# One scatter per tile, a first fold by thirds on VectorE, and tables loaded in the expert stage: one change to a fused attention, experts and Fourier-mixing kernel

## The chip, the cores and the metric

The kernel runs on one core of a Trainium2 chip as one launch. The metric is the device time of that launch in microseconds (us), the median of three runs. A core has five engines with an instruction stream of their own, each in order: TensorE (PE; its weight loads are shown as PEld), VectorE (DVE), ScalarE (ACT), GpSimd (POOL) and SyncE (SP), which here only issues DMA transfers. They meet through semaphores. On-chip data lie in SBUF and PSUM (what TensorE writes); everything else is DRAM.

## What is computed

Three layers over 4 sequences of 576 tokens, 8 heads of 64, model width 512:

```python
# attention: per query only the 32 largest scores are kept
scores = scale * q @ k.T;  kth = the 32nd largest score of each row
attn = softmax(where(scores >= kth, scores, -1e9));  x = attn @ v
# experts: a token's expert is its own argmax, or that of the token before it
e = argmax(logits[b, s]) if s == 0 or local_gate[b, s] < 0.5 else prev_e
out[b, s] = softmax(logits[b, s])[e] * (relu(x[b, s] @ w1[e]) @ w2[e])
# mixing
u = x + real(fft(fft(x, axis=1), axis=2))
un = (u - mean(u)) / sqrt(var(u) + 1e-6)
return u + relu(un @ w_ch1) @ w_ch2
```

All of it is float32. Matrix products are done in three parts: each operand is split into a high part, which TensorE takes without loss, and the rest (low), and high x high, high x low and low x high are added up in PSUM.

## The kernel before

The body is one program with a hand-written order: every engine executes its instructions in the order in which the Python code emits them, and a framework adds the semaphores that the data and the buffers ask for (a buffer of a ring can be written only when its last reader is done).

**Attention** (to about 555 us) ends with each token's row scattered into `xs_d`, sorted by expert. With the row go its weight and, as numbers, the rows of `xm_d` into which its expert's output has to go; they come from a table made in `_tables`. `xm_d` holds per sequence two halves of 289 rows: tokens 1 to 288 and 0 in the one, tokens 575 down to 288 and 0 in the other. The halves are folded later (row n of one with row n of the other), so tokens 0 and 288 stand in both, and a token has up to two target rows.

**Expert stage** (560 to 821 us). Eight experts in order of size, with room for 512, 384, 368, 352, 320, 288, 256 and 256 tokens (`CAPS`); each is 8 steps over the hidden width. A step emits `mm1` (up-projection of 128 hidden units for all tokens of the expert: 12 matmuls, then ScalarE's relu and VectorE's low part) and, two steps later, `mm2` (down-projection into one PSUM bank per tile of 128 tokens, three products). `finish` (L1043) scales the tiles into `ysb`, by ScalarE and VectorE in turn, and `store` (L1058) scatters them with an indirect DMA of GpSimd: per tile two, one for each half of `xm_d`, where the rows without a target in that half are left out by a bounds check; 46 in all. Beside this run: the splitting of the next expert's weights (`raw` to `whi`, `wlo`, L213 and L214), the loads of `xs_d`, the load of the transform's table `tst` (L1094, GpSimd's queue, step 2), and the conversion of the mixing weights, one piece of 128 x 512 in four steps (`f64_step`, L1001: ScalarE L938, VectorE L939 to L946, a store of `fa`, two buffers).

**Transform** (L1183 to L1306). The two-dimensional transform's real part is computed from folded inputs. For each of 4 sequences (batch b): `load_x` brings the two halves `xa` and `xb` in three pieces of 112, 112 and 65 rows (SyncE, two buffers); `fold` makes xa + xb (VectorE: `fe`) and xa - xb (GpSimd: `fo`) and folds each again along the 512 features, first for pieces 0 and 1 together, then for piece 2; `parts` splits both into high and low (`eh`, `el`, `oh`, `ol`). `over_tokens` is one of 5 passes of 9 matmuls with the table `tst` (three from the even fold, two from the odd), each evacuated by ScalarE (high) and VectorE (low) from one of three PSUM buffers. `over_features` is one of 3 blocks of 15 matmuls with the tables `tct` and `tnt`; VectorE's two results go to `md_d`. The next batch's fold is emitted among the passes and blocks of the current one. Ahead of the loop stand the loads of batches 0 and 1, two loads of 1 MB of mixing weights (`m1`), and, on GpSimd behind the first fold, the loads of `tct` and `tnt` (L1280, L1281).

**Mixing** (L1310 on). 2304 tokens in 9 groups of 256. `load_u(g)` brings a group's rows of `md_d` and `xm_d`, and `norm(g)` gives five pieces of work: `add` (GpSimd, two additions into `ut`), `ln` for each half (VectorE with one ScalarE step), and `tr` for each half (four transposes on TensorE, ScalarE's high and VectorE's low part, one PSUM buffer). The hidden width is taken in 4 quarters; a step (quarter q, group g, f) emits `mm1` (12 matmuls), and `mm2` of the step before (6 matmuls; after f = 3 the result is added into `ut`). In quarter 0 the norm of group g + 2 is spread over the steps of group g (f = 3: `add`) and g + 1 (f = 0 to 3: `ln`, `ln`, `tr`, `tr`). The norm of group 0 is done in batch 3 of the transform, its transposes behind feature blocks 0 and 1; group 1's load, norm and transposes come at the head of the mixing:

```python
load_u(1, cp)
nops = norm(1, cp); nops.pop(0)()     # then one piece per step, from step 0
```

## Time and profile before

| | us |
|---|---|
| median of three runs | 1348.8 (1345.58 to 1350.65) |
| the profiled execution, whole | 1346.73 |
| its span (first to last instruction) | 1344.9 |
| busy in the span: TensorE, VectorE, ScalarE, GpSimd | 1210.7, 914.2, 696.3, 572.9 |

The profile is one execution. All its times are counted from the start of the span. A row of the timeline has the start, the duration, the engine, the line, the operation with its output and inputs by tile name, and in brackets how long the engine was idle before it and what ended that. Rows of the chain of waits follow what ended last, backwards. Rows by stage give, for each stretch, the busy time of each engine, the TensorE clock as a share of full speed (0.50 and 1.00 are its two levels, 1.2 and 2.4 GHz), the share of time in which the DMA engines were busy, and what they moved.

### The profile page before, as it was taken

The numbers are of one execution on the slowest core, as the hardware profiler recorded it, in microseconds if no ns is written. First come the engines' busy times: TensorE is split into PE (matmuls) and PEld (weight loads), VectorE is DVE, ScalarE is ACT, GpSimd is POOL, SyncE is SP. The second block draws the span as 40 slices with busy tenths as digits, with TensorE's granted clock in tenths as the row PEclk, the third lists the DMA queues.
The fourth block names the chain that finished last, engine by engine and source line by source line (L and its number), as shares of the span: only waits on it lengthen the run. The fifth ranks groups of instructions, "written<-read, shape, count | busy, mean of one in ns | idle before, by whom it ended". The sixth has DMA issues, their size and how long they took to land.

```text
span 1344.9 us, 25588 instructions
## 1 busy us (share of the span) xinstructions
PE 1210.7 (90%) x8601; PEld 1088.2 (81%) x8601; DVE 914.2 (68%) x3555; ACT 696.3 (52%) x1750; POOL 572.9 (43%) x745
## 2 busy tenths in 40 slices
PE   5999889899899987499999994887999999999996
PEld 4999778888788786389888883776888999999995
DVE  7999899999999997365666673764654444443222
ACT  6999888898899886144444551232322222221110
POOL 5888787987798776302212232642210000000111
PEclk8999989998999899599999997898999999999998
DMA  4656433433444212575666774743230100100111
GB/s 108 184 145 191 121 81 88 109 88 75 101 101 103 50 23 100 187 242 181 216 218 226 229 269 103 211 143 92 83 126 1 62 33 32 63 1 1 48 48 48
DMA packets 128966, 152.29 MB, mean 113 GB/s; under 512 B 69919, under 2 KB 74263, under 8 KB 128712
## 3 DMA queue, kind: packets, MB, share of 16 engines
q1 hardware_dynamic: 122008, 133.34, 34.3%
q0 software_dynamic: 6816, 17.22, 3.7%
q8 instruction: 69, 1.13, 0.3%
q14 instruction: 73, 0.60, 0.1%
HBM read 92.05 MB, written 38.39 MB: 97 GB/s over the span
## 4 chain that ended last, share of the span: by engine, by line
DVE 30%; PE 29%; issue 21%; POOL 11%; DMA 5%; ACT 2%; SPq 1%; POOLq 0%; DVEq 0%; ACTq 0%
PE f L1368 11%; PE f L1352 11%; DVE cd L432 8%; DVE y L463 5%; POOL xm_d L828 4%; DVE sc L469 3%; DMA xs_d<-xtok,ix 3%; PE u L536 2%; DVE cw L443 2%; DVE lo L329 2%; DVE cw L445 1%; POOL y L458 1%; POOL fo L1209 1%; PE s L411 1%; DVE mt L442 1%
## 5 line engine op out<-in xcount | busy, mean ns | idle before, releaser
L432 DVE MAX8 cd<-ss 128x8 f32<-128x72 f32 x1152 | 215.7, 217 | 1.2 <-ACT ss L426 1.0
L1357 DVE SCALAR_TENSOR_TENSOR fhl<-f,fhh 128x256 fp32r<-128x256 f32 x144 | 60.9, 423 | 211.8 <-ACT fhh L1356 211.8
L536 PE MATMUL u<-in_v,et 128*128 128x74 f32 (+1 forms) x1600 | 191.6, 270 | 10.0 <-ACT st_x L543 9.0
L1356 ACT ACTIVATE fhh<-f 128x256 fp32r<-128x256 f32 x144 | 55.3, 384 | 277.4 <-PE f L1352 277.4
L536 PEld LDWEIGHTS u<-in_v,et 128*128 128x128 f32 (+1 forms) x1600 | 182.0, 185 | 19.8 <-ACT st_x L543 15.3
L458 POOL TENSOR_TENSOR y<-ss,g 128x576 f32<-128x576 f32 x144 | 185.1, 1286 | 22.7 <-ACT st_x L543 7.8
L504 POOL TENSOR_TENSOR z<-ss,mt 128x576 f32<-128x576 f32 x144 | 168.7, 1171 | 14.9 <-DVE cd L432 9.8
L1377 POOL DMA_INDIRECT out_dram<-ut,orow x18 | 17.6, 977 | 318.4 <-DVE ut L1373 316.5
L517 PE MATMUL tp<-ident,z 128*128 128x128 f32 x576 | 120.8, 289 | 16.4 <-DVE lo L329 14.7
L453 ACT ACTIVATE g<-ss,mt 128x576 bf16<-128x576 f32 x144 | 118.9, 826 | 29.7 <-DVE mt L446 28.1
L828 POOL DMA_INDIRECT xm_d<-ysb,sid x46 | 49.4, 1073 | 195.9 <-ACT ysb L1052 187.4
L411 PE MATMUL s<-kt,qp 128*128 128x288 f32 x640 | 127.2, 327 | 3.4 <-DVE qp L360 1.6
L495 ACT ACTIVATE bb<-ss,kb 128x576 bf16<-128x576 f32 x144 | 116.7, 810 | 8.7 <-POOL kb L474 8.7
L463 DVE MAX8 y<-y 128x8 f32<-128x576 f32 x144 | 106.7, 741 | 10.9 <-POOL y L458 10.8
L426 ACT ACTIVATE ss<-s 128x288 f32<-128x288 f32 x288 | 111.6, 464 | 4.2 <-PE s L411 2.7
L518 PE MATMUL tp<-neg_id,bb 128*128 128x128 bf16 x576 | 109.3, 224 | 3.9 <-ACT bb L495 3.9
L517 PEld LDWEIGHTS tp<-ident,z 128*128 128x128 f32 x576 | 87.4, 152 | 27.0 <-POOL y L458 7.7
L411 PEld LDWEIGHTS s<-kt,qp 128*128 128x128 f32 x640 | 95.9, 200 | 6.6 <-ACT kt L361 3.1
L1352 PEld LDWEIGHTS f<-nxh,whi 128*128 128x128 f32 x576 | 88.2, 189 | 14.2 <-issue 1.2
L214 DVE TENSOR_TENSOR wlo<-raw,whi 128x1024 fp32r<-128x1024 f32 x70 | 85.5, 1260 | 19.7 <-ACT whi L213 19.5
L1368 PE MATMUL f<-whi,fhh 128*128 128x512 f32 x288 | 92.3, 402 | 0.6 <-ACT fhh L1356 0.6
L1352 PE MATMUL f<-nxh,whi 128*128 128x256 f32 x576 | 91.5, 280 | 1.0 <-DVE dd L1266 1.0
(256 smaller groups left out, 2972.8 us busy)
## 6 DMA issues: line engine op xcount, KB each, us to landing
raw<-in_moe_w_dram SPq DMA_DIRECT2D x32, 1024.0 KB
kt<-hi SPq DMA_DIRECT2D x60, 144.0 KB
kt<-lo SPq DMA_DIRECT2D x60, 144.0 KB
xs_d<-xtok SPq DMA_DIRECT2D x8, 1056.0 KB
fr<-in_moe_w_ch_dram SPq DMA_DIRECT2D x16, 512.0 KB
raw<-in_moe_w_ch_dram SPq DMA_DIRECT2D x16, 512.0 KB
md<-md_d SPq DMA_DIRECT2D x9, 516.0 KB
in_k<-in_k_dram SPq DMA_DIRECT2D x32, 128.0 KB
```

The costliest lines, as they stand in the source:

```text
L411: PE.matmul(p, QP[i][:, s, o:o + 128].bitcast(F32R), KT[i][j][:, s, c].bitcast(F32R), start=(s == heads[0] and j == 0), stop=(s == heads[- ...
L426: ACT.activation(t[:, 288 * hf:288 * hf + 288], SPS.pop((n, hf)), AF.Copy)
L432: return [lambda j=j: DVE.max(cd[:, 8 * j:8 * j + 8], SS[n][:, 72 * j:72 * j + 72]) for j in range(8)]
L453: ACT.activation(g, SS[n], AF.Sign, bias=MT[i][:, t, 1, 7:8], scale=-SCL, accum_out=DIF[n])
L458: POOL.tensor_tensor(y, SS[n], LT[n], op=OP.mult)
L463: DVE.max(y8, Y8[n])
L495: ACT.activation(t, SS[n], AF.Relu, bias=KB.pop(n), scale=-HUGE)
L504: POOL.tensor_tensor(ZZ[n], SS[n], bcast(MT[i][:, t, 0, 0:1], [128, S]), op=OP.subtract)
L517: PE.matmul(o, z[:, k], ident, start=True, stop=False, is_transpose=True)
L536: PE.matmul(p[0:m, s, 0:VW], et[:, kc, qs], vv[:, kc, VC[s]], start=(kc == 0), stop=(kc == 4))
L1352: PE.matmul(p, a[:, d, fs], x[:, d], start=(n == 0), stop=(n == 11))
L1368: PE.matmul(yp[c], a[:, c * 128:(c + 1) * 128], w[:, f, :], start=(f == 0 and n == 0), stop=(f == 3 and n == 2))
```

## The change

1. A token's output goes to one row of `xm_d` only. The table has one target, `store` and the overflow path issue one scatter per tile (23 for 46), and `load_x` reads two halves of 287 rows plus, into both halves, the two rows of tokens 288 and 0.
2. In the last step of an expert `mm2` goes tile by tile instead of product by product.
3. `tct` and `tnt` move to the pool of `tst`; their loads are emitted in the expert stage, at step 10, on GpSimd's queue. To make room `fa` has one buffer.
4. Batch 0 is folded by a new function, `first`: all on VectorE, piece by piece, the even half before the odd one, with ScalarE's high parts between. The load of batch 1 is issued behind the first addition (a transfer of one element that reads its result holds SyncE's queue), and the two loads of mixing weights stand behind the load of batch 2.
5. Groups 0 and 1 are loaded at the start of batch 2 and normalised in batches 2 and 3, their transposes behind passes 2 and 3 and feature blocks 0 and 1 of batch 3. The mixing starts with the load of group 2, and the pieces for group g are placed at steps 4g - 7 (`add`), 4g - 6 and 4g - 5 (`ln`), 4g - 3 and 4g - 2 (`tr`).

```diff
@@ _tables
-                if s <= S // 2:
-                    lay[p, 5 * b + t, 1] = b * 2 * NS + (s - 1) % NS + 1
-                if s == 0 or s >= S // 2:
-                    lay[p, 5 * b + t, 2] = b * 2 * NS + NS + (S - s - 1 if s else NS - 1) + 1
+                lay[p, 5 * b + t, 1] = b * 2 * NS + ((s - 1) % NS if s <= S // 2 else NS + S - s - 1) + 1
...
@@ expert stage
     tst = tp_.tile([112, 3, 4, 290], F32R, name="tst")
+    tct = tp_.tile([128, 3, 2, 258], F32R, name="tct")
+    tnt = tp_.tile([128, 2, 2, 258], F32R, name="tnt")
...
-                FA[i] = mp.tile([128, 512], F32, name="fa", bufs=2)
+                FA[i] = mp.tile([128, 512], F32, name="fa", bufs=1)
...
-            for n, (a, w) in enumerate(((hh, wh), (hh, wl), (hl, wh))):
-                for c in range(nt):
-                    m = min(128, CAPS[r] - 128 * c)
-                    PE.matmul(YP[r][c][0:m], a[:, c * 128:c * 128 + m], w[:, f % 4, :],
-                              start=(f == 0 and n == 0), stop=(f == 7 and n == 2))
+            order = [(n, c) for n in range(3) for c in range(nt)]
+            if f == 7:
+                order.sort(key=lambda o: o[1])
+            for n, c in order:
...
-                for a in range(2):
-                    st = to_rows(sid[0:m, a, c:c + 1], ysb[0:m, c])
+                st = to_rows(sid[0:m, c], ysb[0:m, c])
...
             if j == 2:
                 POOL.dma_start(tst, ts)
+            if j == 10:
+                POOL.dma_start(tct, tcd)
+                POOL.dma_start(tnt, tnd)
@@ transform
+            x = xm_d[2 * b * NS:(2 * b + 2) * NS].rearrange("(g n) d -> g n d", g=2)
             for g, t in enumerate(XA[b]):
-                x = xm_d[(2 * b + g) * NS:(2 * b + g + 1) * NS]
-                SP.dma_start(t[:, 0:2], x[0:224].rearrange("(j p) d -> p j d", p=112))
-                SP.dma_start(t[0:65, 2], x[224:289])
+                SP.dma_start(t[:, 0:2], x[g, 0:224].rearrange("(j p) d -> p j d", p=112))
+                SP.dma_start(t[0:63, 2], x[g, 224:287])
+
+            for t in XA[b]:
+                SP.dma_start(t[63:65, 2], x[0, 287:289])
...
+        def first():
...
+            def add(j, i):
+                m, op = DT[j], (OP.add, OP.subtract)[i]
+                t = fs[i][0:m, j % 2]
+                DVE.tensor_tensor(t, xa[0:m, j], xb[0:m, j], op=op)
+                DVE.tensor_tensor(t[:, 1:256], t[:, 1:256], t[:, 511:256:-1], op=op)
+                ACT.activation((eh, oh)[i][0:m, j], t[:, 0:(258, 256)[i]], AF.Copy)
+
+            def low(j, i):
+                m, n = DT[j], (258, 256)[i]
+                DVE.tensor_tensor((el, ol)[i][0:m, j], fs[i][0:m, j % 2, 0:n], (eh, oh)[i][0:m, j].bitcast(F32), op=OP.subtract)
+
+            for i in range(2):
+                add(0, i)
+                if i == 0:
+
+                    SP.dma_start(fp.tile([1, 1], F32, name="after", bufs=1), fs[0][0:1, 0, 0:1])
+                    load_x(1)
+                add(1, i)
+                low(0, i)
+                add(2, i)
+                low(1, i)
+                low(2, i)
+
         load_x(0)
-        load_x(1)
-        for load, _ in m1:
-            load()
-        for i in range(2):
-            fold(0, i)
-            parts(0, i)
-        POOL.dma_start(tct, tcd)
-        POOL.dma_start(tnt, tnd)
+        first()
         nops = []
         for b in range(B):
             more = b + 1 < B
-            if b == 2:
-                load_u(0, lp)
-            if b == B - 1:
-                nops = norm(0, lp)
+            if b == B - 2:
+                for g in range(2):
+                    load_u(g, lp)
+                n0, n1 = norm(0, lp), norm(1, lp)
+                nops = [n0[:1], n0[1:2], n0[2:3], [n0[3], n1[0]], [n0[4], n1[1]], n1[2:3], n1[3:4], n1[4:5]]
             for c in range(5):
                 over_tokens(b, c)
                 if more and c == 1:
                     fold(b + 1, 0)
-                if len(nops) > 2:
-                    nops.pop(0)()
+                if b == B - 1:
+                    for o in nops.pop(0):
+                        o()
             if b + 2 < B:
                 load_x(b + 2)
+            if b == 0:
+                for load, _ in m1:
+                    load()
             for j in range(3):
                 over_features(b, j)
...
-                if nops and j < 2:
-                    nops.pop(0)()
+                if b >= B - 2 and j == 2 or b == B - 1 and j < 2:
+                    for o in nops.pop(0) if nops else ():
+                        o()
@@ mixing
-        load_u(1, cp)
+        load_u(2, cp)
         steps = [(q, g, f) for q in range(NQ) for g in range(NG) for f in range(4)]
...
+        nops, later = {}, {}
+        for g in range(2, NG):
+            if g > 2:
+                nops.setdefault(4 * g - 9, []).append(lambda g=g: load_u(g, cp))
+            nops.setdefault(4 * g - 7, []).append(lambda g=g: later.update({g: norm(g, cp)}))
+            for k, at in enumerate((7, 6, 5, 3, 2)):
+                nops.setdefault(4 * g - at, []).append(lambda g=g, k=k: later[g][k]())
...
                 if q == 0:
-
-                    if f == 0 and g + 2 < NG:
-                        load_u(g + 2, cp)
-                    if nops:
-                        nops.pop(0)()
-                    if f == 3 and g + 2 < NG:
-                        nops = norm(g + 2, cp)
-                        nops.pop(0)()
+                    for o in nops.pop(i, ()):
+                        o()
```

## Rows read from the trace of the kernel before

**Rows 1.** Busy time by stage (each engine's us and instructions, PE clock, DMA share, GB/s):

```profile
560.00:830.00 270.00, 260.51 (x1409) 225.45 (x1408) 164.08 (x256) 122.63 (x190) 58.49 (x95) 0.98 0.64 215
830.00:849.00 19.00, 6.43 (x23) 5.18 (x24) 8.57 (x9) 2.80 (x6) 11.22 (x9) 0.50 0.98 270
...
1021.00:1345.00 324.00, 312.79 (x2007) 281.89 (x2005) 125.41 (x250) 61.68 (x143) 19.17 (x36) 0.99 0.09 35
```

**Rows 2.** Timeline at the end of the experts: start, us, engine, line, operation:

```profile
820.57 0.63 PE L1040 MATMUL m<-whi,hl 128*128 128x512 f32 x2
...
821.97 0.97 POOL L828 DMA_INDIRECT xm_d<-ysb,sid  x1 [14.72 <-ACT ysb L1052]
```

**Rows 3.** Chain of waits from experts to transform (start, us, what was waited for):

```profile
825.80 2.27 DMA xm_d<-ysb,sid
...
829.40 6.63 DMA xb<-xm_d
```

**Rows 4.** Timeline of the first fold, VectorE beside GpSimd:

```profile
837.40 2.71 DVE L1210 TENSOR_TENSOR fe<-fe 112x510 f32<-112x510 f32 x1
```

**Rows 5.** Instructions by line in the whole span (ns, minimum/median/maximum; first, last start):

```profile
L1208 DVE TENSOR_TENSOR fe<-xa,xb x8: 689/1514/2830, 836.1 to 885.0; 112x1024 f32<-112x1024 f32 x4, 65x512 f32<-65x512 f32 x4
...
L1222 DVE TENSOR_TENSOR el<-fe,eh x8: 424/689/1095, 841.0 to 888.6; 112x516 fp32r<-112x516 f32 x4, 65x258 fp32r<-65x258 f32 x4
```

**Rows 6.** Timeline of the transform: TensorE's first table matmul, batches 1 and 3, GpSimd's fold:

```profile
854.68 0.47 PE L1254 MATMUL pc<-tct,ch 86*112 86x258 f32 x2 [2.52 <-DMA tct<-in_tab_c_dram]
...
861.75 0.44 PE L1240 MATMUL p<-tst,eh 112*86 112x290 f32 x2
...
866.11 2.14 POOL L1211 TENSOR_TENSOR fo<-fo 112x510 f32<-112x510 f32 x1
...
886.97 0.44 PE L1240 MATMUL p<-tst,eh 112*86 112x290 f32 x2
```

**Rows 7.** Timeline of batch 3, three engines:

```profile
891.26 0.43 PE L1240 MATMUL p<-tst,eh 65*86 65x290 f32 x2
...
891.39 0.82 DVE L1243 TENSOR_TENSOR cl<-p,ch 86x290 fp32r<-86x290 f32 x2
892.28 0.69 DVE L1162 BATCH_NORM_STATS2 bs<-ut 128x6 f32<-128x512 f32 x1
...
896.28 0.55 DVE L1169 TENSOR_SCALAR md<-ut,mv,rs 128x512 f32<-128x512 f32 x1
...
891.16 1.09 POOL L1158 TENSOR_TENSOR ut<-ut,md 128x510 f32<-128x510 f32 x1
```

**Rows 8.** Timeline of the mixing's head; TensorE, GpSimd's sum, VectorE's normalisation:

```profile
903.46 0.71 PE L1352 MATMUL f<-nxh,whi 128*128 128x256 f32 x4 [0.99 <-DVE dd L1266]
...
911.05 1.27 POOL L1157 TENSOR_TENSOR ut<-ut,md 128x514 f32<-128x514 f32 x1 [18.80 <-DMA ut<-xm_d]
...
918.18 0.90 PE L1175 MATMUL lt<-ident,md 128*128 128x128 f32 x3 [2.23 <-DVE md L1169]
...
929.76 1.60 DVE L1169 TENSOR_SCALAR md<-ut,mv,rs 128x512 f32<-128x512 f32 x1
...
939.88 0.63 PE L1352 MATMUL f<-nxh,whi 128*128 128x256 f32 x4
...
1018.53 0.63 PE L1352 MATMUL f<-nxh,whi 128*128 128x256 f32 x4
```

**Rows 9.** Timeline of the expert stage: table load, a wait for weights, fa:

```profile
577.20 0.62 POOL L1094 DMA_DIRECT2D tst<-in_tab_s_dram x1
...
589.83 2.01 ACT L213 ACTIVATE whi<-raw 128x1024 fp32r<-128x1024 f32 x2 [4.67 <-DMA raw<-in_moe_w_dram]
...
795.03 0.43 SPq L1012 DMA_DIRECT2D c_d<-fa  x1
...
799.57 0.67 ACT L938 ACTIVATE fa<-fr 128x512 f32<-128x512 f32 x1
```

**Rows 10.** DMA issues (out, in, queue, count, KB each, us from issue to landing):

```profile
tst<-in_tab_s_dram POOLq DMA_DIRECT2D x1, 1522.5 KB, 9.1
```

More of the change, by code (lines that the diff above doesn't have):

```diff
@@ L894, in overflow @@
                 SP.dma_start(xo, xs_d[bass.ds(slot, 128), :])
-                ix = op.tile([128, 2], I32, name="oix")
-                om = op.tile([128, 2], F32, name="om_")
-                rows_of(ix, xo[:, DM + 2 * IW:XW:IW], om)
+                ix = op.tile([128, 1], I32, name="oix")
+                om = op.tile([128, 1], F32, name="om_")
+                rows_of(ix, xo[:, DM + 2 * IW:DM + 2 * IW + 1], om)
                 xt = op.tile([128, 4, 128], F32, name="xt")
@@ L913, in overflow @@
                 ACT.activation(yo, p, AF.Copy, scale=xo[:, DM:DM + 1])
-                for a in range(2):
-                    to_rows(ix[:, a:a + 1], yo)
+                to_rows(ix, yo)
     slow = nc.values_load(slow_i[0:1, 0:1], min_val=0, max_val=1)
@@ L973, in prep @@
             pv = mp.tile([128, XCAP // 128, 1], F32, name="pv", bufs=2)
-            sid = mp.tile([128, 2, XCAP // 128], I32, name="sid", bufs=2)
-            em = mp.tile([128, 2, XCAP // 128], F32, name="em", bufs=1)
+            sid = mp.tile([128, XCAP // 128, 1], I32, name="sid", bufs=2)
+            em = mp.tile([128, XCAP // 128, 1], F32, name="em", bufs=1)
             XH[r] = (xh, xl, pv, sid)
@@ L980, in f @@
                     DVE.tensor_copy(pv[:, 0:nt], XS[r][:, 0:nt, DM:DM + 1])
-                    rows_of(sid[:, :, 0:nt], XS[r][:, 0:nt, DM + 2 * IW:XW:IW].rearrange("p c a -> p a c"), em[:, :, 0:nt])
+                    rows_of(sid[:, 0:nt], XS[r][:, 0:nt, DM + 2 * IW:DM + 2 * IW + 1], em[:, 0:nt])
                 p = ps.tile([128, XCAP], F32, name="tp", bufs=2)
@@ L1036, in mm2 @@
             wh, wl = W[r, f // 4, 1]
-            for n, (a, w) in enumerate(((hh, wh), (hh, wl), (hl, wh))):
-                for c in range(nt):
-                    m = min(128, CAPS[r] - 128 * c)
-                    PE.matmul(YP[r][c][0:m], a[:, c * 128:c * 128 + m], w[:, f % 4, :],
-                              start=(f == 0 and n == 0), stop=(f == 7 and n == 2))
+            order = [(n, c) for n in range(3) for c in range(nt)]
+            if f == 7:
+                order.sort(key=lambda o: o[1])
+            for n, c in order:
+                a, w = ((hh, wh), (hh, wl), (hl, wh))[n]
+                m = min(128, CAPS[r] - 128 * c)
+                PE.matmul(YP[r][c][0:m], a[:, c * 128:c * 128 + m], w[:, f % 4, :],
+                          start=(f == 0 and n == 0), stop=(f == 7 and n == 2))
         def finish(r):
@@ L1061, in store @@
                 m = min(128, CAPS[r] - 128 * c)
-                for a in range(2):
-                    st = to_rows(sid[0:m, a, c:c + 1], ysb[0:m, c])
-                    for o in prev_sc:
-                        tc.declare_no_dep(st.ins, o.ins, reason="every token has its own rows")
-                    prev_sc.append(st)
-                    POOL.memset(spacer, 0.0)
+                st = to_rows(sid[0:m, c], ysb[0:m, c])
+                for o in prev_sc:
+                    tc.declare_no_dep(st.ins, o.ins, reason="every token has its own row")
+                prev_sc.append(st)
+                POOL.memset(spacer, 0.0)
         load_slots(0)
@@ L1185, in body @@
         ps = ph.enter_context(tc.tile_pool(name="dft_ps", bufs=1, space=PSUM))
-        tct = fp.tile([128, 3, 2, 258], F32R, name="tct")
-        tnt = fp.tile([128, 2, 2, 258], F32R, name="tnt")
         XA, FE, EO, CS = {}, {}, {}, {}
@@ L1271, in over_features @@
                 SP.dma_start(md_d[r + NS:r + NS + m, h], dd[0:m, 1 - h])
-        load_x(0)
-        load_x(1)
-        for load, _ in m1:
-            load()
-        for i in range(2):
-            fold(0, i)
-            parts(0, i)
-        POOL.dma_start(tct, tcd)
-        POOL.dma_start(tnt, tnd)
+        def first():
+            EO[0] = [fp.tile([112, 3, n], F32R, name=nm, bufs=1)
+                     for nm, n in (("eh", 258), ("el", 258), ("oh", 256), ("ol", 256))]
+            eh, el, oh, ol = EO[0]
+            xa, xb = XA[0]
+            fs = [fp.tile([112, 2, DM], F32, name=nm, bufs=1) for nm in ("fe", "fo")]
+            def add(j, i):
[17 more added lines that the diff above has]
+                low(2, i)
+        load_x(0)
+        first()
         nops = []
```

3 lines of the change are left out of this document (removed).

## The prediction

> **What bounds the kernel now.** I read the table by stage first [rows 1]. In the expert stage TensorE is busy 260.5 of 270 us and in the last three quarters of the mixing 312.8 of 324, both near full clock: work taken off other engines is worth nothing there. Between experts and transform, 830 to 849, it is busy 6.4 of 19 us at half clock. So the change can pay only in three places: the gap behind the experts, the transform's first batch, and the head of the mixing. The timeline gives the gap: the experts' last matmul ends at 821.2, and the first of four scatters starts at 821.97 [rows 2]. The chain of waits goes on through the fourth, at 825.80, which lands 2.27 us later, and then through the load of xb, issued at 829.40 and landed at 836.03 [rows 3]. The fold follows on VectorE and GpSimd, beside each other, where a step of VectorE's takes up to 2.71 us [rows 4]. TensorE then waits once more, until 854.68, for the table tct; batch 1 starts at 861.75 and batch 3 at 886.97 [rows 6]. The mixing starts at 903.46, idles for the sums and normalisation of group 1 (its sum starts at 911.05, its transposes resume at 918.18) and reaches group 2 at 939.88 and group 8 at 1018.53 [rows 8].
>
> **A. Experts to data.** With the last down-projection sorted by tile, tile 0 is complete three matmuls, about 0.7 us, earlier, so the first scatter starts near 821.3. Four scatters lie (825.80 - 821.97) / 3 = 1.28 us apart; with two, the last starts at 822.55, 3.25 us earlier. It now writes all its rows where it wrote about half: 131 KB more at the 270 GB/s of [rows 1] is 0.5 us, so landing takes 2.7 us (bounds 2.27 and twice that; nearer the first, since most of 2.27 can't be data). Loads then start 2.8 us earlier, at 825.7. Before, the part of batch 0 that the fold needs (1.03 MB) came 7.5 us after the first issue, with 3.2 MB of batch 1 and mixing weights queued behind and sharing the engines. Those are now held back. Alone, 1.03 MB at 270 GB/s is 3.8 us, plus the 2 us that a small transfer shows: 5.8 us (5.5 if it is faster, 7.5 if sharing cost nothing). Data at 831.5 instead of 836.0: **4.5 us** (1 to 5.5). The two extra row loads are 4 KB behind the rest and cost two issues of SyncE with nothing to feed; the mixing weights, moved behind batch 2's load, are needed only in the mixing, and hide under three batches.
>
> **B. First fold.** VectorE now does it alone. Its shortest 512-wide addition is 0.69 us and its shortest 258-wide difference 0.42 [rows 5]; beside GpSimd 510 elements took 2.71 [rows 4]. A third costs 0.69 + 0.42 + about 0.06 of dependence = 1.17, its low part 0.42; three thirds of the even half 4.9, both halves 9.75 us after the data. TensorE's three even passes (1.2 us each at full clock, twice that at half) run beneath the odd half; the two odd ones run from 10.25 to 12.65. VectorE meanwhile evacuates two passes (10.6), folds batch 1's first piece in about 3 beside GpSimd (whose second step takes 2.14 [rows 6], its first no less: 14.3), and evacuates the other three passes: 14.8. Feature block 0 thus ends at 15.0, with tct long loaded, and two more blocks of 1.85 put batch 1 at 18.75 us after the data, where it was 25.7. Batch 1's load is issued behind the first addition, at 1.8, and is in by about 8, before it is wanted at 9.75. The table's removed wait of 2.5 us is not worth 2.5: VectorE's evacuations also ended at 854.6. A and B: batch 1 at 850.25 instead of 861.75, **11.5 us** (7 to 14). Batches 1 and 2 stay at 12.6 each, as measured (25.2 from 861.75 to 886.97): five passes of 1.2, three blocks of 1.85 and a microsecond of waits.
>
> **C. Tables and single buffers in the expert stage.** GpSimd has nothing between the issue of tst at 577.20 [rows 9] and the first scatter, so both tables go out right behind it, not at their step: 1290 KB more while tst takes 9.1 us for 1522 KB [rows 10], 167 GB/s. That is 7.7 us of a shared path. The weights that ScalarE waited for until 589.83 [rows 9] come up to 3.9 us later if they lose half of it. Their result is due at TensorE six or more us after that, so it is covered; uncovered it would cost up to 3. The Trainium skill (DMA: Bandwidth & Descriptors, section "Queues, rings and completion order") says that each DMA engine takes turns between the queues with work; tst's 167 GB/s, on engines that move 270 elsewhere [rows 1], agrees; if the weights went first instead, this part would be 0. The single fa makes ScalarE's next range step wait for the store: in the tightest expert the store is issued at 795.03 and the step starts at 799.57 [rows 9]. 4.5 us against 0.26 MB behind 0.5 MB (2.8 at 270 GB/s, plus 2) is a tie; ScalarE has about 1 us of idle behind it and TensorE a step of 2.8. Loss **0.5 us** (0 to 3). Halving 46 scatters frees GpSimd, which nothing waits for there.
>
> **D. Batch 3 carries two groups.** This is where I expect a loss. VectorE reaches batch 3's first evacuation at 891.39, 4.4 us after the batch began, because GpSimd and VectorE still fold; GpSimd's sum for group 0 ends at 892.25 [rows 7]. So group 0's second normalisation ends no earlier than 896.8 [rows 7], 9.9 us in. TensorE finishes the third pass 4.7 us in [rows 7]. Before, the transposes stood behind the feature blocks; now the first stand between pass 2 and pass 3, and TensorE, in order, has to stand still from 4.7 to about 10. GpSimd's sum for group 1 now runs just then, and such a normalising step took 1.60 us beside GpSimd instead of 0.55 [rows 7, 8]: 10.9 us in. Behind it VectorE is the bound: 0.69 for each transposed half, 0.44 for each evacuation, two normalisations of about 2 us (the first here starts at 892.28, the second's last step ends at 896.83, with one evacuation between [rows 7]) for group 1, with TensorE's half clock after the wait (0.9 us of it on the path): group 1's second ends near 19.5, its first transposes hold feature block 1, and the mixing starts at 25.3 instead of 903.46 - 886.97 = 16.5. **Loss 8.8 us** (4 to 11). Its worth is that groups 0 and 1 are ready.
> The Trainium skill (SBUF — State Buffer, section "Who interferes with whom") says that a VectorE operation using both ports and a GpSimd one block each other wholly, and issue order decides. The 1.60 agrees; if VectorE were first each time, the sum would lose 1 us less.
>
> **E. Head of the mixing.** From 903.46 to group 2 at 939.88 were 36.4 us [rows 8]. A step is 2.8 us (312.8 us of [rows 1] are 111 steps and a half); eight, less the first down-projection, are 21.0, group 2's transposes 0.9, the wait for the last transform stores that the first step keeps 0.6. Group 2's sum can start as group 1's did, 7.6 us behind the first matmul (8.0, one load more); sum and normalisation take 4.4, and the evacuation queued behind it on VectorE comes 1.1 us late. 23.6 us: **12.8 gained** (11 to 13.5). **Then** the order: the transposes waited a step behind a normalisation that GpSimd's sum slowed [rows 8]; now two steps lie between. 24 steps of 2.8 and twelve transposes of 0.46 are 72.8 against 78.65 from 939.88 to 1018.53: **5.85 gained** (4 to 6).
>
> **Sum.** 11.5 - 0.5 - 8.8 + 12.8 + 5.85 = 20.8, on the profiled execution's 1346.7 us (span 1344.9 and 1.8 around it): 1325.9. That execution lies 2.1 below the median of 1348.8, so I predict 1348.8 - 20.8 = **1328 us**.
>
> **Rivals.** (1) The transposes in batch 3 don't hold TensorE, because the fold's end, shifted, leaves VectorE free earlier: D shrinks to about 1 us, 1320. For it: in batch 3 only the fold's tail, 4.4 us, delays the first evacuation; against: that fold is ordered among batch 2's passes, as before, so its tail moves with them. (2) The entrance gains half: the first load is no faster alone and the expert stage loses 3: 11.5 falls to 6, 0.5 rises to 3, 1336. For it: the engines move no more than 270 GB/s in any case. (3) Nothing much: batch 3's wait drops TensorE's clock for the rest of the batch (6 us more) on top of (2): 1343, within the bound of no change. The Trainium skill (TensorE: Matmul & The Clock Gate, section "HAM oscillation") says that an idle TensorE restarts at 1.2 GHz; rows of this kernel agree, the gap of 830 to 849 standing at 0.50 [rows 1]. (4) Slower: the single fa. Each of 15 steps makes ScalarE, and through the up-projection's evacuation TensorE, wait for a store; from 1.4 us each on TensorE's path it eats the whole gain, and at 1.8 it gives 1348.8 - 20.8 + 27 = 1355. Against it: ties of under 1 us with 2.8 us of cover. (5) The load waits on something else than the scatters, so that A is nil and the rest stands: 1332, inside the forecast's own range.
>
> **How the numbers follow.** Forecast with (5) 0.65, (1) 0.12, (2) 0.13, (3) 0.06, (4) 0.04. The forecast's own range by its bounds is 1322 to 1335; with (1) and (2), each with a couple of microseconds of its own, it is 1318 to 1340, which leaves out (3) and (4), 1 in 10, and 1 in 10 of sizes. 0.5%, 6.7 us, is about what a measurement of this kernel can tell from no change: faster 0.90, same 0.06, slower 0.04.
>
> **What would show it.** Right: last scatter near 822.5; batch 0's xb in by 832; batch 1's first pass about 11 us earlier; a wait of TensorE of some 5 us for the normalised group before pass 3 of batch 3; no wait for group 1 in the mixing, and groups of 12.1 us there. Wrong: a wait on ScalarE before its range step that reaches TensorE; batch 1's fold waiting for its load; batch 3 no longer than 17 us; the mixing's first steps waiting on group 2 for more than 3.

## The result and the profile after

The changed kernel takes 1327.25 us (median of four runs, 1324.5 to 1330.88); the kernel before, timed beside it, 1349.62 (1345.58 to 1350.65). The ratio is 0.9843, 95% interval 0.9815 to 0.9871. The profiled execution of the changed kernel took 1326.02 us, with a span of 1324.2. The forecast was 1328, range 1318 to 1340, so the time fell as forecast. Not all terms of the sum came out.

The stages of the changed kernel, as [rows 1] shows those of before (us, busy us and instructions of each engine, granted clock of TensorE, DMA share, GB/s):

```profile
core 0: us, PE busy (x) PEld busy (x) DVE busy (x) ACT busy (x) POOL busy (x), PEclk, DMA share, GB/s
820.08:830.60 10.52, 0.00 (x0) 0.00 (x0) 0.81 (x3) 0.02 (x1) 2.10 (x4) 0.64 0.47 145
830.60:840.00 9.40, 7.00 (x27) 6.17 (x27) 8.78 (x19) 3.10 (x8) 0.00 (x0) 0.50 0.51 134
840.00:850.20 10.20, 10.20 (x46) 9.96 (x45) 8.15 (x10) 2.66 (x6) 6.19 (x4) 0.50 0.97 320
852.60:877.94 25.34, 24.28 (x183) 22.88 (x182) 21.20 (x35) 9.45 (x24) 17.32 (x11) 1.00 0.66 196
877.94:903.38 25.44, 17.54 (x109) 15.99 (x107) 16.51 (x37) 8.98 (x21) 6.96 (x7) 0.80 0.29 93
903.38:927.15 23.77, 22.62 (x146) 20.21 (x147) 11.21 (x25) 4.81 (x13) 4.67 (x4) 1.00 0.44 139
927.15:999.62 72.47, 72.47 (x482) 66.03 (x481) 48.22 (x96) 22.87 (x51) 14.17 (x10) 1.00 0.27 91
```

They are the gap behind the experts, batch 0 (two rows, to shortly before batch 1 at 852.60), batches 1 and 2, batch 3, the mixing's head and its groups 2 to 7. TensorE's granted clock stays at 0.50 (1.2 GHz of its two levels) until 850.3, though from 840 on it is busy without a pause; batch 3 holds a loss of clock and of work (17.5 of 25.4 us busy); from group 2 on TensorE never stops. The way into the transform, in the timeline (start, duration) and then in the chain of waits:

```profile
821.66 0.97 POOL L825 DMA_INDIRECT xm_d<-ysb,sid  x1 [0.23 <-issue]
824.58 0.33 SPq L1199 DMA_DIRECT2D xa<-xm_d  x1
830.60 0.69 DVE L1288 TENSOR_TENSOR fe<-xa,xb 112x512 f32<-112x512 f32 x1 [6.11 <-DMA xb<-xm_d]
840.48 3.02 DVE L1212 TENSOR_TENSOR fe<-xa,xb 112x1024 f32<-112x1024 f32 x1
852.60 0.43 PE L1244 MATMUL p<-tst,eh 112*86 112x290 f32 x2
```

```profile
821.66 2.53 DMA xm_d<-ysb,sid
825.42 5.09 DMA xb<-xm_d
834.76 10.20 PE p L1244 x40
```

In the kernel before, the load and the fold stood here:

```profile
828.50 0.32 SPq L1198 DMA_DIRECT2D xa<-xm_d  x1
836.15 1.22 DVE L1208 TENSOR_TENSOR fe<-xa,xb 112x1024 f32<-112x1024 f32 x1 [14.15 <-DMA xb<-xm_d]
```

Against these and [rows 2, 3] there are two scatters, the last at 821.66 instead of 825.80; the load is issued at 824.58 instead of 828.50 and the fold starts at 830.60 instead of 836.15. Where the chain of before ran through GpSimd's fold, 10.2 us of it are now TensorE's own passes. Batch 3:

```profile
884.74 1.05 DVE L1172 TENSOR_SCALAR md<-ut,mv,rs 128x512 f32<-128x512 f32 x1
885.85 0.48 PE L1178 MATMUL lt<-ident,md 128*128 128x128 f32 x1 [3.01 <-DVE md L1172]
888.14 0.90 PE L1178 MATMUL lt<-ident,md 128*128 128x128 f32 x3 [1.81 <-DVE md L1172]
897.82 0.55 PE L1178 MATMUL lt<-ident,md 128*128 128x128 f32 x3 [1.40 <-DVE md L1172]
903.38 0.72 PE L1386 MATMUL f<-nxh,whi 128*128 128x256 f32 x4 [0.99 <-DVE dd L1270]
```

TensorE stands 6.2 us for transposes whose input VectorE has not normalised. In the expert stage ScalarE's longest waits (us, times, longest) are these:

```profile
ACT whi L210 <- DMA raw<-in_moe_w_dram: 8.6, 1, 8.6
ACT fa L934 <- DMA c_d<-fa: 1.3, 1, 1.3
```

### The profile page after: what moved, and what is told of

Same layout as the page of the kernel before. It is cut to its first block, busy times and chain, and to the rows that moved or that the text cites. A ratio compares the mean times of both kernels' runs of the same rounds, so it can differ in the third digit from the quotient of the medians.

```text
span 1324.2 us, 25516 instructions
## 1 busy us (share of the span) xinstructions
PE 1209.5 (91%) x8601; PEld 1090.9 (82%) x8601; DVE 917.2 (69%) x3567; ACT 695.9 (53%) x1752; POOL 535.2 (40%) x693
## 5 line engine op out<-in xcount | busy, mean ns | idle before, releaser
L533 PE MATMUL u<-in_v,et 128*128 128x74 f32 (+1 forms) x1600 | 188.9, 268 | 14.9 <-ACT st_x L540 9.6
L455 POOL TENSOR_TENSOR y<-ss,g 128x576 f32<-128x576 f32 x144 | 184.9, 1284 | 24.1 <-ACT st_x L540 10.3
L825 POOL DMA_INDIRECT xm_d<-ysb,sid x23 | 23.6, 1025 | 219.2 <-ACT ysb L1053 215.8
L521 ACT ACTIVATE et<-tp 128x512 f32<-128x512 f32 x144 | 91.8, 637 | 4.0 <-PE tp L515 4.0
```

Of the source, the lines that this page charges most:

```text
L455: POOL.tensor_tensor(y, SS[n], LT[n], op=OP.mult)
L533: PE.matmul(p[0:m, s, 0:VW], et[:, kc, qs], vv[:, kc, VC[s]], start=(kc == 0), stop=(kc == 4))
```

## How the stages are compared

All times below come from timelines by the same marks: start and end of TensorE's work on the experts, VectorE's first addition (data), the first matmul of batches 1 and 3, of the mixing, of group 2 and of group 8. Kernels that don't differ in a stage repeat groups 2 to 7 to 0.03 us, the experts and the way to the data to about 1 us, the mixing's head to 0.8, and batch 0 (data to batch 1) only where the clock rises at the same time. The start of the experts alone lies between 555.0 and 564.2 us in the fourteen profiles. No part of the change or of an experiment touches what is ahead of that. So a difference of some microseconds is read from stages, and the whole time decides only between large ones. Us, one profile each; a kernel that ran only once has no ratio:

| kernel | experts | experts to data | data to batch 1 | batches 1, 2 | batch 3 | mixing to group 2 | groups 2 to 7 | ratio to before |
|---|---|---|---|---|---|---|---|---|
| before | 262.1 | 14.95 | 25.60 | 25.22 | 16.49 | 36.42 | 78.65 | |
| changed | 262.4 | 10.52 | 22.00 | 25.34 | 25.44 | 23.77 | 72.47 | 0.9843 |
| e4_together | 262.6 | 10.82 | 21.94 | 25.31 | 25.42 | 23.73 | 72.46 | 0.9840 |
| e11_mfirst | 263.2 | 10.73 | 25.45 | 25.38 | 26.80 | 23.52 | 72.46 | |
| e3_both | 262.8 | 11.30 | 25.72 | 25.62 | 25.45 | 23.87 | 72.45 | 0.9890 |
| e2_warm | 262.9 | 11.04 | 22.05 | 25.28 | 25.45 | 23.19 | 72.44 | 0.9858 |
| e9_warm2 | 262.3 | 10.47 | 19.55 | 26.55 | 26.97 | 23.75 | 72.43 | |
| e5_tabs | 262.9 | 11.08 | 23.99 | 24.76 | 25.46 | 23.06 | 72.45 | |
| e1_order | 262.6 | 10.67 | 22.01 | 25.34 | 20.71 | 24.46 | 72.45 | 0.9817 |
| e8_later | 263.0 | 10.94 | 19.56 | 26.52 | 19.97 | 25.55 | 72.44 | 0.9841 |
| e13_best | 262.5 | 10.85 | 21.04 | 25.07 | 18.31 | 27.55 | 72.45 | 0.9817 |
| e14_bw | 262.5 | 10.48 | 19.55 | 26.55 | 18.33 | 27.75 | 72.44 | 0.9857 |
| e15_room | 262.4 | 11.56 | 21.04 | 25.36 | 16.53 | 23.89 | 72.44 | 0.9804 |
| e6_mix | 262.3 | 10.96 | 21.04 | 25.37 | 26.76 | 23.17 | 77.65 | |

The intervals of the ratios are 0.002 to 0.006 to either side. All edits are to the changed kernel.

## Experiments on the load (A)

**e4_together**

```
         load_x(0)
+        load_x(1)
+        for load, _ in m1:
+            load()
         first()
...
-                    SP.dma_start(fp.tile([1, 1], F32, name="after", bufs=1), ...)
-                    load_x(1)
```

> The changed kernel with batch 1's load and the first mixing weights issued right behind batch 0's load, as in the kernel before, instead of behind the first addition and behind batch 2's load. Theory (3.2 MB on the same engines slows the load that the fold waits for): data 7.5 us after the first issue instead of 5.9, so everything behind it 1.6 us later, time 1328.9; nothing else moves. Rival (the load is limited by itself): 5.9 to 6.2 us, time 1327.3, and then the 1.1 us more of the load's shortening is of another cause.

Measured: 6.32 us from the first issue to the fold, 10.82 from the experts' end, within the 10.52 to 11.56 of the runs that left this stage alone, whose same load took 6.02 us (changed kernel) to 7.05 (e15_room). The rival holds: no cost of issuing batch 1's load early is shown. The kernel before's 7.65 lies outside that spread, but it is one profile. SyncE, however, held four pieces of that load back, by up to 1.3 us, and issued the weights only at 829.31, behind the data at 828.38.

**e11_mfirst**

```
         load_x(0)
+        for load, _ in m1:
+            load()
         first()
```

> The changed kernel with the first two mixing weights (2 MB) issued right behind batch 0's load, ahead of batch 1's. With batch 1's load there instead, part of it held back by SyncE's own waits, the data came 6.3 us after the first issue (6.0 as changed, 7.65 before). Theory (sharing slows the load that the fold waits for, by what is really in flight beside it): with 2 MB at once behind it 7.0 to 7.7 us. Rival (the load is limited by itself, and the kernel before was slow by the form of its load): 6.0 to 6.4 us.

Measured: 6.25 us to the first addition, as the rival has it. The sharing shows elsewhere: the first addition needs only the two large pieces, issued at 827.04 and 827.89; the last third of the batch, whose smallest pieces were issued at 828.67 and 828.97 just ahead of the weights at 829.28, came late:

```profile
840.31 0.69 DVE L1288 TENSOR_TENSOR fe<-xa,xb 65x512 f32<-65x512 f32 x1 [4.48 <-DMA xa<-xm_d]
```

So 2 MB close behind a load do slow its tail: VectorE waits 4.5 us for it, and batch 1 comes 3.45 us later than in the changed kernel. Holding the weights back is worth something; holding batch 1's load back is not shown to be. Why the first addition had its data 7.65 us after the issue in the kernel before and 6.0 to 7.05 in all thirteen profiles here stays open: the form of the load (65 rows in one piece, now 63 and 2) changed too and was not tried alone.

## Experiments on the first fold and the clock (B)

**e3_both**

```
         load_x(0)
-        first()
+        fold(0, 0)
+        SP.dma_start(fp.tile([1, 1], F32, name="after", bufs=1), FE[0, 0][0][0:1, 0, 0:1])
+        load_x(1)
+        parts(0, 0)
+        fold(0, 1)
+        parts(0, 1)
```

> The changed kernel with its first batch folded by VectorE and GpSimd beside each other, in two pieces, as in the kernel before; loads, tables and the mixing as changed. Theory (as the prediction had it: the fold by thirds is worth something, and the table's wait of the kernel before was only worth what VectorE's evacuations left of it, under 1 us): batch 1 starts 25 us after the data (22.0 as changed, 25.6 before), time 1330. Rival 1 (the whole gain of 3.6 us came from the tables that no longer arrive late): 22.5 us or less, time 1327.5. Rival 2 (the fold alone is worth more than it seemed, since the half clock eats it too): over 26 us, over 1331.

Measured: 25.72 us, between the theory and rival 2, and as long as in the kernel before (25.60), though the wait for the table is gone. Here the clock stood at 0.50 until 861.2, in the changed kernel until 850.3, in both cases until 2 to 3 us before batch 1; with nearly all of batch 0 at half clock in both, the fold by thirds is worth 3.7 us at batch 1 and, with batches 1 and 2 added, 4.0 at batch 3. What the table's wait itself was worth in the kernel before can't be read from this, since the clock there rose earlier.

**e2_warm**

```
         load_x(0)
+        pw = lps.tile([128, 2, GT_], F32, name="lt")
+        for _ in range(84):
+            PE.matmul(pw[0:128, 0, 0:256], tst[:, 0, 0, 0:128], tst[:, 0, 0, 0:256], start=True, stop=True)
         first()
```

> The changed kernel with 84 matmuls more, whose result nobody reads, on TensorE in the gap between the experts' last matmul and the transform's first (about 820.5 to 831.5 us). Theory (batch 0 is late because TensorE works it at half clock until about 850): with the clock at 1.00 the 9-matmul passes take 1.2 us instead of 2.2 and a feature block 1.9 instead of 3.2, and batch 1 starts 18.8 us after the data (the predicted value; 22.0 in the changed kernel), so that the time falls by 3.2 us, to 1324. Rival (VectorE's chain of folds and evacuations sets batch 0, the clock only fills its pauses): batch 1 stays at 21.5 to 22 us after the data and the time at 1327. If the dummy work runs at half clock itself it ends late, and the first pass starts later than 1.9 us after the data.

Measured: 22.05 us, no gain, but not for the rival's reason (columns as above):

```profile
826.30:836.60 10.30, 10.28 (x84) 10.12 (x84) 0.19 (x2) 0.00 (x0) 1.56 (x4) 1.00 0.52 148
836.60:838.30 1.70, 0.03 (x1) 0.00 (x0) 1.63 (x4) 0.42 (x1) 0.00 (x0) 1.00 0.00 0
838.30:840.60 2.30, 1.41 (x5) 0.72 (x5) 2.16 (x5) 0.74 (x2) 0.00 (x0) 0.70 0.69 159
840.60:856.20 15.60, 15.57 (x66) 15.28 (x67) 13.09 (x21) 4.60 (x12) 6.31 (x4) 0.50 0.87 257
```

The clock was full through the filling and the 1.70 us behind it, fell inside the first pass, and then stayed at 0.50 for 15.6 us of unbroken work. The run does not tell the two theories apart; the next one does.

**e9_warm2**

```
+                    if b == 0 and n % 3 == 2:
+                        warm({0: (4, 10, 4), 3: (0, 12, 4)}.get(c, (0, 0, 0))[j])
                     PE.matmul(p[0:dm], x[0:m, j, d0:d0 + dm], tst[0:m, j, y, :], start=(n == 0), stop=(n == 8))
...
+        warm(98)
         first()
```

> The changed kernel with unread matmuls not only in the gap (98) but also between the thirds of the first even and the first odd pass, where TensorE waits for VectorE; in the run with the gap alone filled (84) the clock was at 1.00 up to the first pass, fell some 1 us into it behind pauses of 1.70, 0.25 and 0.65 us, and batch 1 still came 22.05 us after the data. Theory (the half clock is what my first-fold step missed): passes of 1.2 us, batch 1 at 18.8 us after the data, 20 if the fold of batch 1's first piece between VectorE's evacuations holds feature block 0. Rival (VectorE sets batch 0): TensorE at 1.00 and batch 1 still at 21.5 or later, with TensorE waiting for VectorE's evacuations. If the clock falls again in spite of the filling, the run tells nothing between the two.

Measured: clock 1.00 throughout batch 0, batch 1 at 19.55 us, which is the theory's second value. The two halves of batch 0 (columns as above), and VectorE's timeline, which says what now holds it:

```profile
831.81:841.50 9.69, 8.22 (x67) 7.95 (x65) 9.07 (x20) 3.41 (x9) 0.24 (x1) 1.00 0.52 139
841.50:851.36 9.86, 9.86 (x79) 9.82 (x80) 9.23 (x11) 2.25 (x5) 6.82 (x4) 1.00 1.03 320
840.96 0.82 DVE L1249 TENSOR_TENSOR cl<-p,ch 86x290 fp32r<-86x290 f32 x2
841.69 3.03 DVE L1212 TENSOR_TENSOR fe<-xa,xb 112x1024 f32<-112x1024 f32 x1
844.76 1.65 DVE L1214 TENSOR_TENSOR fe<-fe 112x510 f32<-112x510 f32 x1
846.33 0.45 DVE L1249 TENSOR_TENSOR cl<-p,ch 86x290 fp32r<-86x290 f32 x1
```

The third evacuation, which feature block 0 needs, stands behind the fold of batch 1's first piece, 4.7 us beside GpSimd. And batches 1 and 2 take 1.2 us longer, all of it in batch 1, where TensorE now waits 0.70 us for the high part of its second piece. From data to batch 3 it is 46.1 us here, 46.1 in e8_later, where the clock rose by itself 13 us after the data and batch 1 came at 19.56, and 47.3 in the changed kernel. So the clock is worth 2.45 us at batch 1 and 1.2 at batch 3. At the mixing nothing is left of it (73.1 us from the data, 72.8 in the changed kernel): batch 3 takes 26.97 us here, with the same three waits for transposes but with a second stretch at 0.50 behind the third of them; e6_mix and e11_mfirst have the same, in 26.76 and 26.80. Where it rose earlier still, TensorE met the same evacuation (e15_room), and the clock fell to 0.50 once more behind the wait:

```profile
850.58 0.37 PE L1258 MATMUL pc<-tct,cl 85*112 85x258 f32 x1 [1.71 <-DVE cl L1247]
```

## Experiment on the tables (C)

**e5_tabs**

```
-            if j == 10:
-                POOL.dma_start(tct, tcd)
-                POOL.dma_start(tnt, tnd)
...
                     load_x(1)
+                    POOL.tensor_copy(fp.tile([1, 1], F32, name="then", bufs=1), fs[0][0:1, 0, 0:1])
+                    POOL.dma_start(tct, tcd)
+                    POOL.dma_start(tnt, tnd)
```

> The changed kernel with the two feature tables loaded behind batch 1's load (issued by GpSimd once VectorE has done the first addition) instead of in the expert stage. Theory (in the expert stage the tables share the DMA engines with the weights, and the delay is covered): ScalarE's longest wait for its raw weights there falls back from 8.6 to 4.7 us, and the stage's 262.4 us stay within 0.5; at the transform the tables' 1.3 MB behind 1 MB need about 9 us from 832 and are wanted at 844.8 in the changed kernel's run, so TensorE waits for them at most 1 us, or up to 3 where the clock rose early. Rival 1 (the tables' place in the expert stage costs what the prediction bounded it by): the stage is 1 to 3 us shorter. Rival 2 (loading them late costs the 2.5 us that the kernel before waited): batch 1 comes 24 us or more after the data.

Measured, in the waits of the expert stage and of batch 0 and in VectorE's timeline:

```profile
ACT whi L210 <- DMA raw<-in_moe_w_dram: 4.0, 1, 4.0
PE pc L1255 <- DVE cl L1244: 0.5, 1, 0.5
847.01 1.23 DVE L1209 TENSOR_TENSOR fe<-xa,xb 112x1024 f32<-112x1024 f32 x1 [2.22 <-DMA xb<-xm_d]
```

ScalarE's wait falls from 8.6 to 4.0 us, and the stage takes 262.9 where the unchanged ones take 262.3 to 263.2: the mechanism is as predicted, and it is covered. TensorE does not wait for the tables. Batch 1 comes at 23.99, which is rival 2's number but not its reason: batch 1's load, now beside the tables, lets VectorE and GpSimd start their fold only at 847.01 and 847.09 (VectorE waits 2.22 us for it), and VectorE's last evacuations stand behind that fold. The two DMA queues thus take from each other, as the Trainium skill has it (DMA: Bandwidth & Descriptors, section "Queues, rings and completion order": each DMA engine goes round between the rows that have work); both traces agree.

## Experiments on batch 3 (D)

The changed kernel's order of the eight steps is `[add0] | [ln0a], [ln0b], [tr0a, add1], [tr0b, ln1a], [ln1b] | [tr1a], [tr1b]`: end of batch 2, five token passes, feature blocks (add: GpSimd's sum; ln: VectorE's normalisation of half a group; tr: transposes).

**e1_order**

```
-                nops = [n0[:1], n0[1:2], n0[2:3], [n0[3], n1[0]], [n0[4], n1[1]], n1[2:3], n1[3:4], n1[4:5]]
+                nops = [n0[:1], n0[1:2], n0[2:3], n1[:1], n1[1:2], n1[2:3], n0[3:4], n0[4:5]]
...
-        nops, later = {}, {}
+        nops, later = {0: n1[3:4], 1: n1[4:5]}, {}
```

> The changed kernel with one thing different: in batch 3 the eight transposes of group 0 go behind feature blocks 0 and 1 instead of between the token passes, and group 1's go behind the first two steps of the mixing. Theory (TensorE, in order, is held by transposes that come too early in its program): its three waits for the normalised group, 3.01 + 1.81 + 1.40 us, go, and so does most of the half clock behind them; batch 3 falls from 25.4 us to 18.5 (17 to 20; 16.5 with one group in the kernel before), the mixing's steps up to group 2 stay at 23.8 plus at most 1, and the time falls by about 6.5 us, to 1320.7. Rival (VectorE is the bound of batch 3 in any order, having two groups to normalise beside GpSimd): batch 3 stays above 23 us and the time above 1325.

Measured: batch 3 20.71 us, head 24.46; 4.0 of the expected 6.5 us. The three waits for transposes are gone; one for an evacuation has come, behind VectorE's normalising step:

```profile
888.47 1.07 DVE L1172 TENSOR_SCALAR md<-ut,mv,rs 128x512 f32<-128x512 f32 x1
889.46 0.44 DVE L1247 TENSOR_TENSOR cl<-p,ch 86x290 fp32r<-86x290 f32 x1
889.96 0.54 PE L1244 MATMUL p<-tst,oh 112*128 112x290 f32 x2 [1.85 <-DVE cl L1247]
```

**e8_later**

```
+                nops = [n0[:1], n0[1:2], n0[2:3], n1[:1], [], [], n0[3:4], n0[4:5]]
...
+        nops, later = {i: n1[i + 1:i + 2] for i in range(4)}, {}
```

> The changed kernel with batch 3 carrying only what it carried in the kernel before (group 0's two normalisations, and its transposes behind feature blocks 0 and 1; of group 1 only GpSimd's sum), and group 1's two normalisations and transposes in the mixing's first four steps. Theory (batch 3 is bound by VectorE's row of normalisations as soon as TensorE no longer stands for the transposes: in the run with the transposes moved it waited 1.85 us for an evacuation behind them and worked the rest at half clock): batch 3 takes 16.5 us or a little less (25.4 as changed, 20.7 with the transposes moved), the mixing up to group 2 takes 23.8 + 0.9 for the transposes, up to 26 if VectorE is late there; both together 41 to 42.5 where the changed kernel has 49.2, and the time about 1320. Rival (GpSimd's second sum is what slows VectorE in batch 3, wherever the rest stands): batch 3 stays above 19, both together above 44.

Measured: 19.97 and 25.55, together 45.5, as the rival has it. The same 1.86 us wait stands there, the next 6 us run at 0.50, and in the mixing a transpose waits 1.44 us for a normalisation. So the number of steps in batch 3 was not what kept it long. The place of the first one, and GpSimd's second sum, were left.

**e13_best**

```
+                nops = [n0[:1], n1[:1], n0[1:2], n0[2:3], [], [], n0[3:4], n0[4:5], n1[1:2]]
...
+        nops, later = {i: n1[i + 2:i + 3] for i in range(3)}, {}
```

> The changed kernel with group 0's two normalisations one token pass later (behind passes 1 and 2, as in the kernel before), its transposes behind feature blocks 0 and 1, group 1's sum right behind group 0's on GpSimd, and group 1's normalisations and transposes at batch 3's end and in the mixing's first three steps. The two earlier orders both gave batch 3 and the mixing's head together 45.2 to 45.5 us (49.2 as changed): in both TensorE waited 1.85 us for the evacuation of pass 1, queued on VectorE behind a normalising step that GpSimd's sum of group 1 stretched to 1.08 us, and worked the next 6 us at half clock. Theory (that one pause and the half clock behind it are all that is left of the loss): batch 3 in 16.5 us (16 to 18), the mixing up to group 2 in 24.7 (24.3 to 25.5), together 41.2; the time 7 to 8 us under the changed kernel's, about 1319.5, ratio to before 0.978. Rival (VectorE has no room for the second group anywhere near): together above 44 again, time 1323, ratio 0.981.

Measured: 18.31 and 27.55, together 45.9: the rival again in sum, but with other waits:

```profile
891.81 0.49 PE L1264 MATMUL pn<-tnt,sh 128*112 128x258 f32 x2 [0.99 <-ACT sh L1246]
906.37 0.75 PE L1178 MATMUL lt<-ident,md 128*128 128x128 f32 x3 [2.77 <-DMA ut<-xm_d]
```

The first is ScalarE's: its evacuation stands behind a square root that waits for VectorE. The second is named for a load, but ends right behind group 1's second normalisation, whose last step ran from 905.77 to 906.32: VectorE had first to wait for the mixing's first evacuation.

**e15_room**

```
+                nops = [n0[:1], n1[:1], n0[1:2], [], [], n0[2:3], n0[3:4], n0[4:5], n1[1:3]]
...
+        nops, later = {1: n1[3:4], 2: n1[4:5]}, {}
```

> The changed kernel with each step of groups 0 and 1 put where VectorE and ScalarE stand idle in the traces so far: group 1's sum right behind group 0's; group 0's first normalisation behind pass 1 and its second behind pass 4 (behind pass 2 its square root kept ScalarE from an evacuation for which TensorE waited 0.99 us); its transposes behind feature blocks 0 and 1; both normalisations of group 1 behind the last block, where VectorE waits over 3 us for the last store of the transform (in the run before, the second one, in the mixing's first step, held TensorE 2.77 us); its transposes in the mixing's second and third steps. Theory (there is room for the second group, each earlier order just met VectorE or ScalarE once more in TensorE's way): batch 3 in 17 us (16.5 to 18.3), the mixing up to group 2 in 24.9 (24.3 to 25.5), together 42 where the changed kernel has 49.2 and the three other orders 45.2 to 45.9. Rival (a new wait takes the place of each removed one): together 45 or more again. The time: 7 us under the changed kernel's by the theory, ratio to before 0.979 with 0.003 of uncertainty from the stages ahead of the experts, which no part of this touches.

```profile
881.99:898.52 16.53, 13.40 (x100) 12.15 (x99) 12.23 (x28) 7.21 (x17) 6.99 (x7) 1.00 0.48 151
898.52:922.41 23.89, 23.31 (x155) 21.13 (x155) 14.80 (x35) 6.59 (x17) 4.87 (x4) 1.00 0.46 138
```

Measured: 16.53 and 23.89, together 40.4 where the changed kernel has 49.2: the theory, and 1.6 better than it. Batch 3 with two sums on GpSimd costs what it cost with one [rows 6, 8], at full clock; so the second sum alone was not the cause either. TensorE still waits 1.39 us in batch 3 and 0.58 us in the head for a normalised half, but the clock does not fall behind these. The time is 1319.73 us (six runs, 1315.78 to 1322.46), ratio 0.9804 (0.9775 to 0.9833): the best of all these kernels by the median. The stages give 8.8 us against the changed kernel, the ratios 0.4%, about 5 us, with intervals that overlap.

**e14_bw** is e13_best with e9_warm2's filling:

```
+                nops = [n0[:1], n1[:1], n0[1:2], n0[2:3], [], [], n0[3:4], n0[4:5], n1[1:2]]
...
+                        warm({0: (4, 10, 4), 3: (0, 12, 4)}.get(c, (0, 0, 0))[j])
...
+        warm(98)
```

> The same with the unread matmuls of the filled gap and first passes as well. Those kept the clock at 1.00 through batch 0 and gave batch 1 at 19.55 us after the data (22.0 in the changed kernel's profiled run, but 19.56 also in a run where the clock rose by itself 13 us after the data), with batches 1 and 2 then 1.2 us longer. Theory (the clock's rise comes at a varying time, and the filling takes the variation out): batch 1 at 19.6, batch 3 at 46.1 after the data, the rest as in the run without it; between nothing and 1.3 us under that run, ratio 0.977. Rival (the filling costs, being in the way of the first passes): the same or slower than without.

Measured: batch 1 at 19.55, batch 3 at 46.10 us after the data, against 21.04 and 46.11 without the filling. What the clock gives batch 0 is all given back by batch 3; its median of 1326.96 was not lower than e13_best's 1323.3.

## Experiment on the mixing (F)

**e6_mix**

```
-            for k, at in enumerate((7, 6, 5, 3, 2)):
+            for k, at in enumerate((7, 6, 5, 3, 2) if g == 2 else (5, 4, 3, 2, 1)):
```

> The changed kernel with groups 3 and on prepared at the mixing steps where the kernel before had them (sum two steps later, normalisation one and two, transposes right behind). Theory (the 6.2 us of groups 2 to 8 come from the two steps that now lie between normalisation and transposes): from group 2 to group 8 78 us (77 to 79; 72.5 as changed, 78.65 before), the time 5 to 6 us more. Rival (they come from something else, such as the scatters' or the loads' place): under 74 us.

Measured: 77.65 us from group 2 to group 8, 5.2 more than 72.47, as the theory has it; the waits for normalised halves are back, six of 0.60 to 0.66 us, of which these are the first two; they are 3.9 of the 5.2 us, and the rest was not traced:

```profile
939.95 0.55 PE L1178 MATMUL lt<-ident,md 128*128 128x128 f32 x3 [0.60 <-DVE md L1172]
952.90 0.55 PE L1178 MATMUL lt<-ident,md 128*128 128x128 f32 x3 [0.65 <-DVE md L1172]
```

## Why the prediction was right, and where not

**A, experts to data: right in sum (4.4 us in this pair, 3.4 to 4.5 by all thirteen profiles; 4.5 predicted).** The last scatter starts 1.6 us behind the experts instead of 4.6 (3.0 of the 3.25), landing grew by 0.26 (0.4), the load took 6.0 us (5.8), which is near the least of its 6.0 to 7.05. But the reason given for the load, that it is alone now, is borne out only for its tail and for the weights; half of rival 2, a load no faster alone, is nearer to what e4_together shows. The 270 GB/s that rival 2 took as the most these engines move is not that: the row of 840.00 to 850.20 shows 320. Rival 5 falls, since the load starts 2.9 us behind the last scatter's start, as before (2.7).

**B, first fold: the term that was mis-sized.** Batch 1 came 22.0 us after the data, not 18.75. VectorE's own fold took its predicted time (the last low part ends 9.2 us after the data, 9.75 predicted). Two things behind it did not: its fold of batch 1's first piece takes 4.7 us beside GpSimd where the sum had 3.7, which puts feature block 0 about 0.8 us later even at full clock (19.55); and the half clock, which the sum let end before the odd passes at 10.25, lasted until 19.7 us after the data in the profiled execution, another 2.45. Half of that is recovered by batch 3, and all of it by the mixing (e9_warm2).

**Batches 1 and 2** took 25.3 us (25.2). **C** cost 0.3 us in this pair (0.5), less than the 0.9 us by which the stage varies, so that no cost is shown: the weights came 3.9 us later, the very figure, and the single fa made one wait of 1.3 us that reached nobody, so the rival of fifteen such waits falls.

**D, batch 3: right in sum (loss 8.95, 8.8 predicted) and in what TensorE waited for.** TensorE stood for transposes between the passes, so that rival 1 falls, VectorE's step was slower beside GpSimd, and the clock fell. One size was off: that step took 1.05 us (0.55 where GpSimd is idle) where the sum had 1.60. Of the half clock, which lasted from 884.4 to 894.7, the sum put 0.9 us on the path; how much really lay there was not separated (TensorE was busy 17.5 us in batch 3, and 13.4 in e15_room at full clock). In e6_mix, e9_warm2 and e11_mfirst, with the same order of steps, the half clock fell into two stretches and the loss was 10.3 to 10.5. The further 6 us of rival 3 did not come (its own sum makes 1342, not 1343). The Trainium skill says that the ports VectorE and GpSimd share are an exclusive lock (SBUF — State Buffer, section "Who interferes with whom"); the 1.05 us beside GpSimd agrees. What the prediction did not say, and e15_room shows, is that none of this loss was needed.

**E and F: right.** The mixing's head takes 23.8 us (23.6), a gain of 12.65; groups 2 to 7 take 72.5 (72.8), a gain of 6.2.

**The sum.** These terms make 17.5 us in the pair of profiled executions (4.4 + 3.6 - 0.1 - 0.3 - 8.95 + 12.65 + 6.2), where the prediction's make 20.8. The executions differ by 20.7. The other 3.2 are 1.4 us by which the experts happened to start earlier and 1.9 by which the program ended sooner behind its last matmul (9.3 us instead of 11.2), less 0.1 in between. The first lies within the spread of 9 us between the profiles; the second is the same in all thirteen profiles of changed kernels. The trace puts it into GpSimd's closing drain, which takes 6.6 us in these and 8.4 in the kernel before; why was not tried. So the forecast's closeness to 1327.25 is in part luck: these 3.2 us make up for what B lost.

## What to carry to other kernels

When work of another stage is slipped into a stage in which engines hand work round, cost not only the work but each engine's queue at the very place: the same steps, ordered five ways, cost batch 3 and the mixing's head 49.2, 45.2, 45.5, 45.9 and 40.4 us. Put the producer's step behind an evacuation that the engine which sets the pace needs next, and the consumer in a step in which its input has long been done. And read small differences by stages with fixed marks, if the stages ahead vary by more than the effect.

## What was not expected of the hardware

TensorE's clock came back after very different stretches of work. In the changed kernel it was at 0.50 from 823.0 until 850.3, the last 15.5 us of them without a pause (also 15.6 us in e2_warm); in e15_room, with the same code there, it rose 8.4 us after the data, and in e8_later 13. In the kernel before it rose 3.6 us after unbroken work began, and fell again behind the next wait. What decides it was not found in these traces, so in a stage that begins behind a gap the time at half clock is a range, not a number.
